# Rebuilding the stored f32 x from its high and low parts in a three-stage kernel (retention, ELU FFN, gated FFN) on one Trainium2 core

## The chip, the cores and the metric

The kernel runs on one core of a Trainium2 chip. The metric is device time in microseconds (us), start to end of one execution; the median of three runs before the change is 871.1 us. Engines are named as in the profile: PE (TensorE matmul), PEld (weight load), DVE (VectorE), ACT (ScalarE), POOL (GpSimd), SP (SyncE, which here only issues DMAs).

## What is computed

```python
def _attn_ref(q, k, v):                  # 4 batches, 8 heads, 576 rows, 64 columns, f32
    scores = np.matmul(q, k.transpose(0, 1, 3, 2)) / sqrt(64)
    gamma = 1.0 - 2.0 ** (-5.0 - np.arange(8))
    Dmat = np.where(rel >= 0, gamma[:, None, None] ** rel, 0.0)
    return np.matmul(scores * Dmat, v)

x = attn_out.transpose(0, 2, 1, 3).reshape(2304, 512)
h = x @ moe_w_in                         # 512 x 2048
x = np.where(h > 0, h, np.exp(np.minimum(h, 0)) - 1) @ moe_w_out
gate = 1 / (1 + np.exp(-(x @ moe2_w_gate)))            # 512 x 1536
out = (gate * (x @ moe2_w_val)) @ moe2_w_out
```

The weights come as 64-bit numbers that are taken apart into f32 on the chip.

## The kernel before

**Precision.** Every f32 operand of a large matmul is kept as a pair: a rounded high part (written by ACT) and the low rest (value minus high part, by DVE or POOL). `mm3` (lines 114 to 116) makes one product of three matmuls: high by high, high by low, low by high. High plus low gives the f32 value back.

**Stages.** Retention runs in 18 steps of 128 rows each (`Step`, `block`), two batches in turn. A step's loads come through SP into one of three `in` buffers or into a borrowed `y` buffer; PE makes scores, sums and outputs (line 274, small 64x64 matmuls), `x_mul` (line 347, DVE) writes the f32 x of the step into an `e` buffer, `x_high` (354, ACT) and `x_low` (361, DVE) split it into `x_of[g]`, where g is the group of four steps (512 rows; group 4 has two steps). For g below 4, `x_low` also sends the f32 x to a DRAM tile `whole[g]` (line 365, 512-byte pieces). Woven in between are the first four of 16 slices of the first FFN (`FF`: `ups`, line 380 or 114 to 116, and, two places later (`LAG`), `downs` into PSUM banks `acc`, emptied by `evac`, lines 440 and 442). The loop over `s` (line 1089) sets that order by hand: `conv[s]` names the weight that is converted there, `loads` the weights requested there, `loads_at` the retention inputs requested in a block, `rest` those that wait until a place's matmuls are done. The places from `begins[1]` (called b, 18) on have 512 columns and no retention any more.

**Pairs of groups.** The other 12 slices of FFN 1 and all of FFN 2 use a seven-product scheme on 2x2 blocks (`Pair`, `product`, `unit`). A pair of row groups needs x blocks "11", "12", "21", "22" and the sums t1 to t4 made of them, each split into high and low. Groups 0 and 1 are the first pair: `prep` loads their four f32 blocks from `whole` into `fs` and `fg` (line 1074) and makes t1 to t4 there (lines 1071, 476, 481, 484). Groups 2 and 3 are the second pair: the split blocks "11", "21", "22" are stored at places b+2 to b+4 (`store`, line 489), t1 to t4 are made later, in the last unit of the first pair, from f32 blocks that `reload` fetches from `whole` (line 992).

**Units.** For each slice pair q from 2 to 7 a `unit_a` runs for the first pair of groups, then again for the second; after that `unit_b` does FFN 2, slice by slice. One unit of the first pair takes 26.5 us. Between a unit's products, `fill` and `bg` put the background work at fixed places: down products, conversions of coming weights (`plan_a`, `plan_b`; `Weight.chain`, lines 154 to 172, with the sums "z" or "s", 196 to 200 and 109, 110), and `hooks`. Converted weights are saved to DRAM tiles `c` (line 1046) and restored for the second pass (1055). `more` (line 961) requests the next raw weight of a list (`feed`) as soon as one of the raw buffers is given back, which is DVE's line 163 of an earlier conversion. Every DMA of these kinds stands in SP's one queue, in program order; a DMA that must wait holds back all behind it.

Of the kernel before, what the change touches and what calls it, by code (L numbers as in the profile page):

```python
# [22 lines left out]
C = 128  # L23
# [20 lines left out]
SPARE = {3: 2, 8: 2, 4: 3, 9: 3, 14: 3}  # L44
LAG = 2
FIRST_APART = 9
WARM = 12, 2, 3, 5, 4, 6


# [5 lines left out]
def retention_elu_glu(  # L55
# [126 lines left out]
    for f in range(FA):  # L182
        for n, src in (("i", w_in), ("o", w_out)):
            i = len(weights)
            W[n, f] = Weight(src[f], i % 8, (0, 0, 1, 1, 0, 1, 0, 1)[i] if i < 8 else t_slot(n, f))
            weights.append(W[n, f])


# [37 lines left out]
    class Step:  # L226
# [16 lines left out]
        def load(self):  # L243
            if self.n in SPARE:
                self.t = spare_y[SPARE[self.n]].rearrange("p (q c) -> p q c", q=NP)
            else:
                self.t = inpool.tile([128, NP, 4 * C], F32, tag="in", name="in")
            self.q, self.kT, self.k, self.v = (self.t[:, :, i * C : i * C + C] for i in range(4))
            if self.last:
                self.load_half(0)  # L250
            elif self.n < FIRST_APART:
                sp.dma_start(out=self.t, in_=ain[self.b, self.c].rearrange("p r x -> r p x"))
            else:
                self.load_pairs(0)
                rest.append(lambda: self.load_pairs(1))
# [4 lines left out]

        def load_half(self, X):
            src = ain[self.b + X, self.c]
            for i in range(2):
                sp.dma_start(out=self.t[:, :, i * C + HC * X : i * C + HC * X + HC],
                             in_=src[:, :, i * C : i * C + HC].rearrange("p q x -> q p x"))
            sp.dma_start(out=self.t[64 * X : 64 * X + 64, :, 2 * C :], in_=src[:, :HC, 2 * C :].rearrange("p t x -> t p x"))

        def scale(self):
            v = self.v.rearrange("t p (h d) -> t p h d", h=2)
# [89 lines left out]

        def x_low(self):  # L360
            dve.tensor_tensor(out=self.x[1], in0=self.xf, in1=self.x[0].bitcast(F32), op=ALU.subtract)
            if self.g < 4:
                if not self.at:
                    whole[self.g] = dpool.tile([128, KB, 512], F32, tag=f"x{self.g}", name="x")
                sp.dma_start(out=whole[self.g][:, :, self.at : self.at + 128], in_=self.xf)


    class FF:
# [78 lines left out]
    class Pair:  # L447
# [2 lines left out]


        HOMES = {"11": (0, 0), "21": (0, 1), "22": (1, 1), "t1": (2, 0), "t2": (2, 1), "t3": (3, 0), "t4": (3, 1)}
        FROM = {"t3": ("22", "12", ALU.subtract), "t2": ("t3", "11", ALU.add), "t1": ("22", "t2", ALU.subtract),
                "t4": ("21", "t2", ALU.subtract)}

# [28 lines left out]
                engine.tensor_tensor(out=p[:, 1, k], in0=self.src[:, k], in1=p[:, 0, k].bitcast(F32), op=ALU.subtract)  # L484

        def store(self, name):
            g, k = {"11": (0, 0), "21": (0, 1), "22": (1, 1)}[name]
            self.halves[name] = dpool.tile([128, 2, KH, 512], F32, tag=f"h{name}", name="h")
            sp.dma_start(out=self.halves[name], in_=x_of[self.g + g][:, :, k * KH : k * KH + KH, :].bitcast(F32))

        def fetch(self, name):
            sp.dma_start(out=self.place(name).bitcast(F32), in_=self.halves[name])
# [309 lines left out]
    with tc.manual_schedule():  # L802
# [50 lines left out]
        for m in range(5, NSTEP):  # L853
            at = {13: 10, 15: 11, 16: 13, 17: 12}.get(m, m - 5)
            loads_at.setdefault(at, []).append(steps[m].load)
        for at, m in ((4, NS - 1), (14, NSTEP - 1)):
            loads_at.setdefault(at, []).insert(0, lambda m=m: steps[m].load_half(1))

        def begin_rest(f):
            while rest:  # L860
                after(rest.pop(0)(), f.end)
# [77 lines left out]
        for i, w in enumerate(weights[4:8]):  # L939
            s = a + 6 + (i * (b - a - 6)) // 4  # L940
            conv[s] = w
            loads.setdefault(s - 2, []).append(w)
        loads.setdefault(b - 7, []).append(W["i", 4])
        for s, n in {-5: ("i", 4), 1: ("i", 5), 2: ("o", 4), 3: ("z", 2), 4: ("o", 5), 5: ("i", 6)}.items():
            conv[b + s] = W[n]

# [11 lines left out]
            feed += [W["2", f]] if f not in EARLY else []  # L958
        feed, last_ones = deque(feed), [W["o", FA - 2], W["o", FA - 1], W["2", FB - 2]]

        def more():
            while raw_free and feed:
                if feed[0] in last_ones and not any(raw_free[0] is r for r in base_raws):
                    if len(raw_free) < 2:
                        return
                    raw_free.rotate(1)
                    if not any(raw_free[0] is r for r in base_raws):
                        return
                feed.popleft().load()
# [19 lines left out]
        def reload(to):  # L989
            for g in (2, 3):  # L990
                to[g] = y_tile(g)
                sp.dma_start(out=to[g], in_=whole[g].rearrange("p k t -> p (k t)"))

        def remake(p):
            return {
# [65 lines left out]
        def prep():  # L1061
            fa, fb = ((lambda t: (t[:, :1024], t[:, 1024:]))(right.tile([128, 2048], F32, tag="s1", name="fs")))
            fc, fd = (right.tile([128, 1024], F32, tag=f"g{i}", name="fg") for i in (4, 5))
            f = {"11": fa, "t2": fa, "12": fb, "t3": fb, "t1": fb, "22": fc, "21": fd, "t4": fd}

            def source(g, k):
                return whole[g][:, k * KH : k * KH + KH, :].rearrange("p k t -> p (k t)")

            def sum(name):
                a, b, op = Pair.FROM[name]  # L1070
                dve.tensor_tensor(out=f[name], in0=f[a], in1=f[b], op=op)

            for name, (g, k) in {"11": (0, 0), "12": (1, 0), "22": (1, 1), "21": (0, 1)}.items():
                sp.dma_start(out=f[name], in_=source(g, k))
            for _ in range(8):
                yield
            for name in ("t3", "t2", "t1", "t4"):
                sum(name)
                yield
                first.high(name, f[name])  # L1080
                yield
                first.low(name, pool if name in ("t3", "t1") else dve)
                yield
                yield
            for name in ("11", "21", "22"):
                first.place(name)

        halves, prepared = None, prep()
        for s in range(end):
# [12 lines left out]
            def stage():  # L1102
                if chain is not None:
                    next(chain, None)
                if s >= begins[1] + 4:
                    next(prepared, None)
            stage()
            if LATE <= s < NSTEP - AHEAD:
# [18 lines left out]
                    stage()  # L1127
            ff[s].ups(stage if s < end - 1 else lambda: None, s, middle, end_)
            if s >= LATE:
                begin_rest(ff[s])  # L1130
            if s == 1:
                w1 = weights[1].chain(dve)
# [22 lines left out]
                begin_rest(ff[s - LAG])  # L1155
            else:
                stage()
            for w in loads.get(s, []):
                load = w.load()
                if s < NSTEP - AHEAD:  # L1160
                    after(load, ff[s - LAG].end)
            save()
            for i, n in enumerate(("11", "21", "22")):
                if s == begins[1] + 2 + i:
                    second.store(n)
            if s == begins[1] + 8:
# [98 lines left out]
        for pair in (first, second):  # L1265
# [3 lines left out]
            for q in range(Q0, QN):  # L1269
                hooks = {}  # L1270
                calls = 7 + len(todo) + (not last_q)
                if not last_q:
# [3 lines left out]
                    if q == QN - 1:  # L1276
                        reload(second.sums)
                        restore(("i", 2 * Q0), ("i", 2 * Q0 + 1), ("z", Q0))
                        p = second
                        hooks = {  # L1280
                            0: [lambda: p.fetch("11")],
                            3: [lambda: p.fetch("21"), lambda: p.sum("t3")],
                            4: [lambda: p.sum("t2")],
                            4.5: [lambda: p.split("t3", dve), lambda: p.sum("t1")],
                            5: [lambda: p.fetch("22"), lambda: p.split("t2", dve)],
                            6: [lambda: p.sum("t4")],
                        }
                    at = (q == Q0 + 1, 1, 2, 3, 4, 4, 6, 6, 7, 7) if len(todo) > 4 else (2, 3, 4, 4)
                else:
                    plan, ahead = ahead[:calls], ahead[calls:]  # L1290
# [15 lines left out]
                    if q + 1 == QN:  # L1306
                        p = y_pair
                        hooks = {
                            1: [lambda: p.high("11")],
                            2: [lambda: p.low("11", dve), lambda: p.sum("t3")],  # L1310
                            4: [lambda: p.sum("t2")],
                            4.5: [lambda: p.split("t3", dve), lambda: p.split("21", pool)],
                            5: [lambda: p.split("t2", dve), lambda: p.sum("t1")],
                        }
                bg = stepper(plan, calls)
                fill = filler(spread(todo, at), bg, hooks)
                unit_a(pair, q, bg, fill, not last_q and q > Q0)
# [26 lines left out]
        for which, pair in enumerate(pairs):  # L1344
            for f in range(FB):
                if not which:
# [5 lines left out]
                    if f == FB - 2:  # L1352
                        unpark((2, 3))
                    plan = plan_b(f)
                else:
                    plan = planned(14)
                back = [(n, f + 1) for n in "vgs" if f + 1 < FB and (which or f + 1 in EARLY)]
# [123 lines left out]
```

## Time and profile before

| | |
|---|---|
| median of 3 runs | 871.1 us (870.54 to 872.78) |
| profiled execution | 868.8 us, span 867.0 us |
| PE | 852.4 us busy, 98% |
| DVE / ACT / POOL | 664.7 / 459.3 / 409.4 us busy |
| DMA | 194.83 MB, mean 225 GB/s |

The profiled execution took 868.8 us, 2.3 us less than the median of the runs shown; its span, 867.0 us, goes from its first to its last instruction. Busy time counts an instruction from start to end, and matmuls overlap, so PE's gaps are read from its waits and from its timeline: 512-column matmuls follow each other there every 0.227 us when nothing holds them. "Issue" as a releaser means that the profile shows nothing that the engine waited for.

### The profile page before, as it was taken

To read this page: it belongs to the slowest core of one execution; us is meant where nothing else is said; L and a number is where in the kernel's file an instruction comes from. 1 tells how busy PE (TensorE), PEld (TensorE's weight loads), DVE (VectorE), ACT (ScalarE), POOL (GpSimd) and SP (SyncE) were. 2 spreads that over 40 slices of the span, in tenths; PEclk is the share of its full clock that TensorE was granted. 3 is DMA by queue.
4 is the path that set the end of the run, shared out by engine and by line. 5 is a ranking of instruction groups with operands and counts; after the bars stand their busy time and mean duration, and the time that the engine had idled before them with its cause. 6 is when DMAs were issued, how large, how long until landed. Compare 5 with 4: busy or idle time off the path is not lost.

```text
span 867.0 us, 16196 instructions
## 1 busy us (share of the span) xinstructions
PE 852.4 (98%) x6375; PEld 728.9 (84%) x6375; DVE 664.7 (77%) x967; ACT 459.3 (53%) x833; POOL 409.4 (47%) x327
## 2 busy tenths in 40 slices
PE   8899999999999999999999999999999999999998
PEld 5798998888888888888878888888888888888886
DVE  5867758789999888887887988589967564777775
ACT  3445475677666666666665665445543344343331
POOL 2445435656546543564552565244543244334453
PEclk9999999999999999999999999999999999999999
DMA  9978628745474696898774765646574665464322
GB/s 339 298 245 245 185 74 314 292 145 202 163 229 184 230 404 227 314 377 274 274 326 176 239 239 210 218 157 196 197 277 157 229 235 194 192 237 170 112 114 98
DMA packets 63852, 194.83 MB, mean 225 GB/s; under 512 B 9888, under 2 KB 19104, under 8 KB 57376
## 3 DMA queue, kind: packets, MB, share of 16 engines
q1 hardware_dynamic: 62512, 192.30, 61.8%
q10 hardware_dynamic: 1264, 1.49, 0.5%
q8 instruction: 50, 0.82, 0.4%
q14 instruction: 26, 0.21, 0.1%
HBM read 127.19 MB, written 66.58 MB: 223 GB/s over the span
## 4 chain that ended last, share of the span: by engine, by line
PE 88%; DVE 4%; DMA 3%; issue 2%; ACT 2%; POOL 1%; SPq 0%; ACTq 0%; DVEq 0%; POOLq 0%
PE u L114 13%; PE u L115 13%; PE u L116 13%; PE acc L114 10%; PE acc L115 10%; PE acc L116 10%; PE tile L114 3%; PE tile L115 3%; PE tile L116 3%; PE to L274 3%; PE h L380 2%; DMA w<-c 2%; PE h L114 1%; PE h L115 1%; PE h L116 1%
## 5 line engine op out<-in xcount | busy, mean ns | idle before, releaser
L110 POOL TENSOR_TENSOR g<-e,g 128x512 fp32r<-128x512 f32 x95 | 133.7, 1412 | 223.8 <-ACT g L109 196.8
L114 PE MATMUL u<-x,s 128*128 128x512 f32 x288 | 112.6, 391 | 0.0
L115 PE MATMUL u<-x,s 128*128 128x512 f32 x288 | 112.3, 390 | 0.0
L116 PE MATMUL u<-x,s 128*128 128x512 f32 x288 | 112.1, 389 | 0.0
L114 PE MATMUL u<-x,w 128*128 128x512 f32 (+1 forms) x264 | 98.3, 372 | 1.5 <-DMA w<-c 1.3
L115 PE MATMUL u<-x,w 128*128 128x512 f32 (+1 forms) x264 | 98.0, 371 | 0.0
L116 PE MATMUL u<-x,w 128*128 128x512 f32 (+1 forms) x264 | 97.7, 370 | 0.0
L109 ACT CAST g<-e 128x512 fp32r<-128x512 f32 x101 | 61.9, 620 | 65.0 <-DVE e L598 39.7
L172 POOL TENSOR_TENSOR w<-t,w 128x512 fp32r<-128x512 f32 x37 | 51.0, 1378 | 41.1 <-ACT w L169 37.5
L114 PEld LDWEIGHTS u<-x,s 128*128 128x128 f32 x288 | 54.1, 188 | 11.5 <-ACT u L522 0.7
L116 PEld LDWEIGHTS u<-x,s 128*128 128x128 f32 x288 | 54.1, 188 | 11.5
L115 PEld LDWEIGHTS u<-x,s 128*128 128x128 f32 x288 | 54.2, 188 | 10.3
L759 DVE TENSOR_TENSOR y<-y,tile 128x512 f32<-128x512 f32 x76 | 51.2, 680 | 10.8 <-PE tile L116 10.6
L114 PE MATMUL acc<-g,w 128*128 128x512 f32 (+1 forms) x168 | 58.2, 346 | 0.4 <-ACT y L440 0.4
L795 DVE TENSOR_TENSOR y<-y,acc 128x512 f32<-128x512 f32 x58 | 39.1, 682 | 25.4 <-PE acc L116 25.0
L114 PEld LDWEIGHTS u<-x,w 128*128 128x128 f32 x264 | 49.8, 189 | 10.2 <-DMA w<-c 1.7
L115 PE MATMUL acc<-g,w 128*128 128x512 f32 (+1 forms) x168 | 57.7, 344 | 0.0
L116 PE MATMUL acc<-g,w 128*128 128x512 f32 (+1 forms) x168 | 57.7, 343 | 0.0
L116 PEld LDWEIGHTS u<-x,w 128*128 128x128 f32 x264 | 49.7, 188 | 8.7
L115 PEld LDWEIGHTS u<-x,w 128*128 128x128 f32 x264 | 49.9, 189 | 7.4
L675 DVE TENSOR_TENSOR y<-y,acc 128x512 f32<-128x512 f32 (+1 forms) x68 | 39.6, 606 | 19.8 <-PE acc L116 17.9
L114 PE MATMUL acc<-w,g 128*128 128x512 f32 (+1 forms) x152 | 54.1, 356 | 0.0
(226 smaller groups left out, 2418.3 us busy)
## 6 DMA issues: line engine op xcount, KB each, us to landing
w<-c SPq DMA_DIRECT2D x72, 512.0 KB, 6.7
c<-w SPq DMA_DIRECT2D x48, 512.0 KB, 4.9
s<-c SPq DMA_DIRECT2D x22, 1024.0 KB, 7.1
c<-s SPq DMA_DIRECT2D x18, 1024.0 KB, 4.9
y<-y SPq DMA_DIRECT2D x8, 1024.0 KB, 6.2
in<-in_ain SPq DMA_DIRECT2D x6, 1024.0 KB, 8.9
raw<-in_w_in SPq DMA_DIRECT2D x12, 512.0 KB, 4.8
in<-in_ain SPq DMA_DIRECT2D x12, 512.0 KB, 5.3
```

Source lines behind the costliest of these rows:

```text
L109: act.copy(hi, src)
L110: lo_engine.tensor_tensor(out=lo, in0=src, in1=hi.bitcast(F32), op=ALU.subtract)
L114: pe.matmul(out_, wh, xh, start=start, stop=False, skip_group_check=shared)
L115: pe.matmul(out_, wh, xl, start=False, stop=False, skip_group_check=shared)
L116: return pe.matmul(out_, wl, xh, start=False, stop=stop, skip_group_check=shared)
L172: lo_engine.tensor_tensor(out=w[:, 1, :], in0=f, in1=w[:, 0, :].bitcast(F32), op=ALU.subtract)
L274: return pe.matmul(out_, w, x, start=start, stop=True, skip_group_check=True)
L380: self.end = pe.matmul(h, w[:, a, c[k]], x[:, b, k, t], start=i + k == 0, stop=i == 2 and k == KB - 1)
L675: dve.tensor_tensor(out=out_, in0=out_, in1=a, op=ALU.add)
L759: dve.tensor_tensor(out=y, in0=y, in1=a, op=ALU.add)
L795: dve.tensor_tensor(out=o, in0=o, in1=a, op=ALU.add)
```

## The change

No step stores its f32 x. `prep` adds high and low of groups 0 and 1 in SBUF instead of loading (two adds on DVE, six on POOL), and its generator starts at place b+2 instead of b+4. For groups 2 and 3, all four split blocks are stored, from b+2 to b+5; in unit q = 3 SP copies the high halves to a DRAM tile `whole[name]`, and in units q = 4 and 5 POOL issues four DMAs that add the low halves onto it; `reload` fetches four 512 KB blocks instead of two of 1 MB. Several requests stand at other places: steps 14 (whole) and 15 and 17 (behind a place's matmuls), the weights 4 to 7 and ("i", 4). Weight 6 uses the other t buffer. The raw loads of ("v", 2) and ("g", 2) are held until the first unit of FFN 2. One split and one sum move from hook 5 to place 12 of the plan of the last `unit_a`.

```diff
+WHOLE, BEHIND = (14,), (15,)
-            W[n, f] = Weight(src[f], i % 8, (0, 0, 1, 1, 0, 1, 0, 1)[i] if i < 8 else t_slot(n, f))
+            W[n, f] = Weight(src[f], i % 8, (0, 0, 1, 1, 0, 1, 1, 1)[i] if i < 8 else t_slot(n, f))
...
             if self.last:
-                self.load_half(0)
-            elif self.n < FIRST_APART:
+                return self.load_half(0)
+            elif self.n in BEHIND:
+                rest.extend(lambda i=i: self.load_pairs(i) for i in range(2))
+            elif self.n < FIRST_APART or self.n in WHOLE:
...
         def x_low(self):
             dve.tensor_tensor(out=self.x[1], in0=self.xf, in1=self.x[0].bitcast(F32), op=ALU.subtract)
-            if self.g < 4:
-                if not self.at:
-                    whole[self.g] = dpool.tile([128, KB, 512], F32, tag=f"x{self.g}", name="x")
-                sp.dma_start(out=whole[self.g][:, :, self.at : self.at + 128], in_=self.xf)
...
+        AT = {"12": (1, 0), "21": (0, 1), "11": (0, 0), "22": (1, 1)}
+        def copy_high(self, name):
+            whole[name] = dpool.tile([128, KH, 512], F32, tag=f"x{name}", name="x")
+            sp.dma_start(out=whole[name], in_=self.halves[name][:, 0])
+
+        def add_low(self, name):
+            pool.dma_start(out=whole[name], in_=self.halves[name][:, 1], accum_op=ALU.add)
+
+        def both(self, name, k, out_, engine):
+            g, h = self.AT[name]
+            hi, lo = (x_of[self.g + g][:, i, h * KH + k, :].bitcast(F32) for i in range(2))
+            engine.tensor_tensor(out=out_[:, k * 512 : k * 512 + 512], in0=hi, in1=lo, op=ALU.add)
...
-        for at, m in ((4, NS - 1), (14, NSTEP - 1)):
-            loads_at.setdefault(at, []).insert(0, lambda m=m: steps[m].load_half(1))
+        loads_at.setdefault(4, []).insert(0, lambda: steps[NS - 1].load_half(1))
+        loads_at[12] = [lambda: rest.append(steps[NSTEP - 1].load)]
+        loads_at[14] = [lambda: rest.append(lambda: steps[NSTEP - 1].load_half(1))]
...
-            loads.setdefault(s - 2, []).append(w)
-        loads.setdefault(b - 7, []).append(W["i", 4])
+            loads.setdefault((4, 6, 7, 13)[i], []).append(w)
+        loads.setdefault(10, []).append(W["i", 4])
...
+        waiting = [W[n, 2] for n in "vg"]
+
         def more():
-            while raw_free and feed:
+            while raw_free and feed and feed[0] not in waiting:
...
-                sp.dma_start(out=to[g], in_=whole[g].rearrange("p k t -> p (k t)"))
+            for name in ("22", "12", "11", "21"):
+                sp.dma_start(out=second.f32(name), in_=whole[name].rearrange("p k t -> p (k t)"))
...
-            for name, (g, k) in {"11": (0, 0), "12": (1, 0), "22": (1, 1), "21": (0, 1)}.items():
-                sp.dma_start(out=f[name], in_=source(g, k))
-            for _ in range(8):
+            for name in ("12", "22", "11", "21"):
+                for k in range(KH):
+                    first.both(name, k, f[name], dve if name == "12" else pool)
+                    yield
+                    if name != "12":
+                        yield
+            for _ in range(2):
                 yield
...
-                if s >= begins[1] + 4:
+                if s >= begins[1] + 2:
                     next(prepared, None)
...
             if s >= LATE:
+                rest.extend(w.load for w in loads.get(s, []))
                 begin_rest(ff[s])
...
-            for i, n in enumerate(("11", "21", "22")):
+            for i, n in enumerate(second.AT):
                 if s == begins[1] + 2 + i:
                     second.store(n)
...
+                    if q in (Q0 + 1, Q0 + 2, Q0 + 3):
+                        by = (second.copy_high, second.add_low)[q > Q0 + 1]
+                        hooks = {j: [lambda n=n, by=by: by(n)] for j, n in zip((1, 3, 5, 6), second.AT) if q == Q0 + 1 or (j < 4) == (q == Q0 + 2)}
...
-                            5: [lambda: p.split("t2", dve), lambda: p.sum("t1")],
                         }
+                        plan[12] = [lambda: p.split("t2", dve), lambda: p.sum("t1"), *plan[12]]
...
+                    if not f:
+                        plan[3] += [waiting.clear, more]
```

The order of PE's instructions is the same before and after. Two places show what moves on the others. First, DVE from the last evacuation of group 4's first pass on (place b+1) to the evacuation before which PE needs the next two banks. Before:

```order
L440 COPY y_2294<-acc 128x256 x2
L157 TENSOR_SCALAR t<-t 128x512
L158 TENSOR_SCALAR t<-t 128x512
L161 ISA t<-raw,t 128x1024
L397 SCALAR_TENSOR_TENSOR e<-e,h 128x512
L163 SCALAR_TENSOR_TENSOR t<-raw,t 128x512
L196 TENSOR_TENSOR t<-t 128x256
L197 TENSOR_TENSOR t<-t 128x256
L199 TENSOR_TENSOR t<-t 128x256
L200 TENSOR_TENSOR t<-t 128x256
L397 SCALAR_TENSOR_TENSOR e<-e,h 128x512
L442 TENSOR_TENSOR y_2294<-y_2294,acc 128x256 x4
```

With the change:

```order
L439 COPY y_2273<-acc 128x256 x2
L501 TENSOR_TENSOR fs<-x_116 128x512
L158 TENSOR_SCALAR t<-t 128x512
L159 TENSOR_SCALAR t<-t 128x512
L501 TENSOR_TENSOR fs<-x_116 128x512
L162 ISA t<-raw,t 128x1024
L396 SCALAR_TENSOR_TENSOR e<-e,h 128x512
L164 SCALAR_TENSOR_TENSOR t<-raw,t 128x512
L197 TENSOR_TENSOR t<-t 128x256
L198 TENSOR_TENSOR t<-t 128x256
L200 TENSOR_TENSOR t<-t 128x256
L201 TENSOR_TENSOR t<-t 128x256
L396 SCALAR_TENSOR_TENSOR e<-e,h 128x512
L441 TENSOR_TENSOR y_2273<-y_2273,acc 128x256 x4
```

The two `fs<-x` rows are high plus low of block "12"; they stand around the two shifts and scalings of a weight's conversion, ahead of all that follows up to the four `y<-y,acc`. On POOL six more such adds stand between the rows behind it.

Second, SP in the last unit before FFN 2 (`w<-c` and `s<-c` restore weights, `c<-x` and `c<-s` save them, `raw` are raw loads). Before:

```order
L1055 DMA w<-c 128x1024 x2
L144 DMA raw<-in_w_val 128x1024
L1055 DMA w<-c 128x1024
L1046 DMA c<-x_116 128x1024
L144 DMA raw<-in_w_gate 128x1024
L1046 DMA c<-x_116 128x1024
L1055 DMA s<-c 128x2048
L1055 DMA w<-c 128x1024 x2
L1046 DMA c<-s 128x2048
L1055 DMA w<-c 128x1024 x2
L1046 DMA c<-x_116 128x1024
L1055 DMA w<-c 128x1024 x2
```

With the change:

```order
L1071 DMA w<-c 128x1024 x3
L1062 DMA c<-x_116 128x1024 x2
L1071 DMA s<-c 128x2048
L1071 DMA w<-c 128x1024 x2
L1062 DMA c<-s 128x2048
L1071 DMA w<-c 128x1024 x2
L1062 DMA c<-x_116 128x1024
L1071 DMA w<-c 128x1024
L145 DMA raw<-in_w_val 128x1024
L145 DMA raw<-in_w_gate 128x1024
L1071 DMA w<-c 128x1024
```

The raw loads of `w_val` and `w_gate` leave the places ahead of the two saves `c<-x`, the restore `s<-c` and all behind them, and stand after the fifth `w<-c` that follows.

## Rows read from the trace of the kernel before

**Rows 1.** The page: span, and PE's busy time.
```profile
span 867.0 us, 16196 instructions
...
PE 852.4 (98%) x6375; PEld 728.9 (84%) x6375; DVE 664.7 (77%) x967; ACT 459.3 (53%) x833; POOL 409.4 (47%) x327
```

**Rows 2.** Waits of PE: total us, times, longest us.
```profile
PE to L274 <- issue: 1.4, 2, 1.2
...
PE u L114 <- DMA w<-c: 1.3, 1, 1.3
...
PE h L380 <- issue: 0.9, 1, 0.9
...
PE acc L114 <- ACT y L440: 0.4, 1, 0.4
...
PE ts L274 <- issue: 0.3, 1, 0.3
```

**Rows 3.** PE's timeline in a late retention step: start us, us, [idle before <-releaser].
```profile
81.28 0.63 PE L274 MATMUL to<-in 64*64 64x64 f32 x29
83.10 0.27 PE L274 MATMUL to<-in 64*64 64x64 f32 x1 [1.19 <-issue]
```

**Rows 4.** Windows: us, busy per engine (x), PEclk, DMA share, GB/s.
```profile
40.00:110.00 70.00, 68.02 (x1759) 64.73 (x1759) 48.27 (x86) 35.66 (x86) 35.27 (x38) 1.00 0.74 224
...
215.50:242.00 26.50, 26.50 (x139) 22.61 (x138) 24.52 (x35) 18.24 (x33) 15.56 (x12) 1.00 0.57 197
...
421.00:428.40 7.40, 7.40 (x34) 6.13 (x33) 7.26 (x10) 2.48 (x5) 3.56 (x3) 1.00 0.26 104
430.50:444.40 13.90, 12.59 (x56) 10.10 (x54) 12.09 (x12) 10.35 (x16) 11.26 (x8) 1.00 1.01 409
```

**Rows 5.** DMA issues: count, KB each, median us to landing.
```profile
w<-c SPq DMA_DIRECT2D x72, 512.0 KB, 6.7
...
x<-e SPq DMA_DIRECT2D x14, 256.0 KB, 4.7
```

**Rows 6.** ACT's timeline, conversion of ("i", 4).
```profile
102.27 0.68 ACT L154 ACTIVATE t<-raw 128x512 f32<-128x512 f32 x1 [1.40 <-POOL w L172]
```

**Rows 7.** Timelines of DVE, POOL and PE around place b+2.
```profile
128.56 1.06 DVE L157 TENSOR_SCALAR t<-t 128x512 f32<-128x512 f32 x1 [0.60 <-ACT t L154]
...
132.01 0.42 DVE L196 TENSOR_TENSOR t<-t 128x256 f32<-128x256 f32 x1
...
133.91 1.40 DVE L199 TENSOR_TENSOR t<-t 128x256 f32<-128x256 f32 x1
...
137.26 1.40 DVE L442 TENSOR_TENSOR y<-y,acc 128x256 f32<-128x256 f32 x4
...
128.04 1.30 POOL L172 TENSOR_TENSOR w<-t,w 128x512 fp32r<-128x512 f32 x1 [0.31 <-ACT w L169]
...
137.78 0.44 PE L114 MATMUL acc<-g,w 128*128 128x512 f32 x1
```

**Rows 8.** DVE's groups from 20 to 460 us: busy us, mean ns | idle before.
```profile
L361 DVE TENSOR_TENSOR x<-e,x 128x512 fp32r<-128x512 f32 x16 | 12.1, 755 | 5.3 <-ACT x L354 5.3
```

**Rows 9.** SP's waits: total us, times, longest us.
```profile
SPq L144 <- DVE t L163: 180.4, 37, 11.1
```

**Rows 10.** Timelines of POOL, SP and PE before the first unit of FFN 2.
```profile
419.13 2.56 POOL L172 TENSOR_TENSOR x<-t,x 128x512 fp32r<-128x512 f32 x2 [3.39 <-ACT x L169]
...
420.45 0.32 SPq L1046 DMA_DIRECT2D c<-x  x1
428.09 0.33 SPq L144 DMA_DIRECT2D raw<-in_w_gate  x1
428.52 0.38 SPq L1046 DMA_DIRECT2D c<-x  x1
...
434.53 0.93 SPq L1055 DMA_DIRECT2D w<-c  x2
...
444.41 0.50 PE L114 MATMUL u<-x,w 128*128 128x512 f32 x1 [1.32 <-DMA w<-c]
```

More of the change, by code (lines that the diff above doesn't have):

```diff
@@ L262, in load_half @@
             src = ain[self.b + X, self.c]
-            for i in range(2):
-                sp.dma_start(out=self.t[:, :, i * C + HC * X : i * C + HC * X + HC],
-                             in_=src[:, :, i * C : i * C + HC].rearrange("p q x -> q p x"))
+            first, _ = [sp.dma_start(out=self.t[:, :, i * C + HC * X : i * C + HC * X + HC],
+                                     in_=src[:, :, i * C : i * C + HC].rearrange("p q x -> q p x")) for i in range(2)]
             sp.dma_start(out=self.t[64 * X : 64 * X + 64, :, 2 * C :], in_=src[:, :HC, 2 * C :].rearrange("p t x -> t p x"))
+            return first
         def scale(self):
@@ L486, in store @@
         def store(self, name):
-            g, k = {"11": (0, 0), "21": (0, 1), "22": (1, 1)}[name]
+            g, k = self.AT[name]
             self.halves[name] = dpool.tile([128, 2, KH, 512], F32, tag=f"h{name}", name="h")
             sp.dma_start(out=self.halves[name], in_=x_of[self.g + g][:, :, k * KH : k * KH + KH, :].bitcast(F32))
+        def copy_high(self, name):
[7 more added lines that the diff above has]
+            engine.tensor_tensor(out=out_[:, k * 512 : k * 512 + 512], in0=hi, in1=lo, op=ALU.add)
         def fetch(self, name):
@@ L1064, in prep @@
             f = {"11": fa, "t2": fa, "12": fb, "t3": fb, "t1": fb, "22": fc, "21": fd, "t4": fd}
-            def source(g, k):
-                return whole[g][:, k * KH : k * KH + KH, :].rearrange("p k t -> p (k t)")
             def sum(name):
@@ L1157, in retention_elu_glu @@
                 stage()
[L1158 to L1161, printed above, removed]
             save()
-            for i, n in enumerate(("11", "21", "22")):
+            for i, n in enumerate(second.AT):
                 if s == begins[1] + 2 + i:
```

## The prediction

> **What bounds the kernel now.** I read the page first. PE is busy for 852.4 of 867.0 us [rows 1], and the change neither adds nor removes nor reorders a matmul. So the change can win back only gaps of PE, some 14.6 us in all, and can lose by making new ones. The list of PE's waits says where the gaps are [rows 2]: apart from the start-up before 40 us, which the change hardly touches, PE waits 1.3 us for a restored weight, 1.4 and 0.3 us for nothing that the profile names ("issue"), and 0.4 us for an evacuation by ACT. PE's timeline shows the largest nameless gap [rows 3]: 29 of 32 equal small matmuls run at once, and the last waits 1.19 us. Nothing in the program tells that matmul from the others, so what was late is likely the instructions themselves, which also come by DMA. Last, the windows [rows 4]: from 40 to 110 us, 68.02 of 70 us of PE are busy, so 1.98 us is all that the retention steps can give. In that stretch the DMA engines are 0.74 busy; between 430.5 and 444.4 us they are full (1.01, at 409 GB/s).
>
> **Stores of x that go.** Sixteen stores of 256 KB leave SP; fourteen of them are in one row [rows 5], 4.7 us to landing each. 16 x 0.262 is 4.2 MB, and 70 us at 224 GB/s [rows 4] are 15.7 MB, so about a quarter of the traffic of the stretch goes. PE waits for no store and no input there [rows 2], so shorter transfers are worth nothing by themselves. What they may be worth is the nameless gaps: 1.19 us [rows 3] and 0.3 us [rows 2]. I take both as gone: -1.19 - 0.3 = **-1.5 us**. Bounds: 0 if they have another cause, and -2.4 us if the 0.9 us nameless gap of the start-up [rows 2], where stores are also in flight, goes too. Inputs and weights that are asked for elsewhere cost nothing while a whole step lies between request and use; PE's 1.98 us of gaps hold no wait for an input. If that cover were gone, one late request costs at most about a landing, 4.7 us [rows 5].
>
> **Other t buffer for weight 6.** Before, ("i", 4) uses the same buffer right behind weight 6, and ACT waits 1.40 us for POOL to finish with it [rows 6]. ACT, then DVE, are late from there on until PE waits 0.4 us for ACT's evacuation [rows 2]. With the other buffer that chain has 1.40 us more room: **-0.4 us**; at worst 0.
>
> **Blocks made in SBUF by prep.** Four loads of 512 KB go, and eight adds come. Six on POOL at about 1.30 us [rows 7] are 7.8 us. At most two of them stand between one g and the next on POOL, so a g comes up to 2.6 us later; PE uses it two places on, 10.9 us later (48 matmuls at 0.227 us). I take that as hidden; all six ahead of one g, 7.8 us, would still be. The two on DVE are another matter. DVE has a single idle of 0.60 us there, before 128.56, and from then on works without a pause (no row has an idle before it) to the evacuation at 137.26, whose first quarter PE awaits at 137.78 [rows 7]: the first of the four parts takes 1.40 / 4 = 0.35 us and so ends at 137.61, 0.17 us before PE uses its bank. PE has next to no room. One such add costs about 0.755 us (same size, both inputs in SBUF [rows 8]). Two are 1.5 us less the idle 0.60: 0.9 us at least, if nothing is stretched. But DVE's work there is stretched beside POOL: two adds of 128x256 take 0.42 and 1.40 us [rows 7]. If both new ones took 1.40 us, the price were 2 x 1.40 - 0.60 = 2.2 us. I take **+1.2 us**, nearer the low end, because 0.755 us is a mean over sixteen, of which some ran beside POOL already. The Trainium skill speaks against this part too: "SBUF — State Buffer", section "Who interferes with whom", says that a DVE instruction with two SBUF inputs contends with a GpSimd instruction that reads SBUF. By that rule alone the price would be the upper end, 2.2 us, and the whole forecast 1.0 us later; the pair 0.42 and 1.40 agrees with the rule, the mean of 0.755 says that not every add pays.
>
> **Fourth store, copies, accumulating DMAs, reload.** The fourth store (1 MB) takes less than the four loads that go (2 MB) in the same stretch. Four copies on SP and four additions issued by POOL come at units q = 3 to 5, where the DMA share is 0.57 [rows 4]; the data are used in unit 7, two units later. On SP they delay no restore there. On POOL the trace has no DMA at all. Bounds: nothing, since in a unit POOL is idle for 26.50 - 15.56 = 10.9 us [rows 4]; or POOL is held until the data have landed, which is the second rival. I take **0**, as an issue on SP holds the queue for 0.3 to 0.4 us [rows 10]. By the Trainium skill ("DMA: Bandwidth & Descriptors", section "Latency and other measured facts") the first byte of a GpSimd DMA comes after about 1 us of emission; by that four cost POOL some 4 us of idle time and the sum stays as it is. The reload in four parts moves as many bytes as in two: 0.
>
> **Held raw loads and moved split.** Before 444.41 PE waits 1.32 us for a weight restore that SP issues at 434.53 [rows 10], into full DMA engines [rows 4]. Just before, from 421 to 428.4, the DMA share is 0.26 [rows 4]: SP's queue stands at the raw load of `w_gate`, issued at 428.09 only, the kind of request that waits for DVE to give back a raw buffer [rows 9]. Behind it stands a save `c<-x`, whose data POOL has finished at 419.13 + 2.56 = 421.7 [rows 10]. With the change the raw load is not there, and the save can start some 6.8 us earlier, in the quiet stretch. So at least 2 x 0.524 = 1.05 MB no longer lie ahead of the late restore; at 409 GB/s that is 2.6 us, twice the wait. **-1.3 us**; bound 0, if the restores behind wait for PE to free their slots, so that nothing but the save comes earlier (0.52 MB, 1.3 us, would still just do). The held loads are issued behind the fifth restore and have until place 11 of 14 of the next unit before they are converted; uncovered they would cost one landing, 6.7 us [rows 5]. The moved split puts a product's add ahead of a split on DVE, in a stretch with no wait of PE before 444.41: 0.
>
> **Sum.** -1.5 - 0.4 + 1.2 + 0 - 1.3 = -2.0 us: the profiled execution of 868.8 us would take 866.8 us. It stands 2.3 us below the median of the runs, 871.1 us; so I put the new median at 871.1 - 2.0 = **869.1 us**, 0.23% less. A measurement of this kernel can tell about 0.3%, 2.6 us, from no change; the forecast lies within it.
>
> **Rivals.**
> *The adds cost nothing.* If DVE takes them up in idle time or the evacuation has more room than the rows show, the gains stand alone: -3.2 us, 867.9 us; with the start-up gap -4.1 us, 867.0 us. For: one idle of 0.60 us is there, and DVE works ahead of PE in other places. Against: no pause from 128.56 to 137.26 [rows 7].
> *POOL is held by its DMAs* (slower). If POOL stands still until its addition has landed, two per unit at 6.7 us (the nearest row of that size, [rows 5]) take 13.4 us out of 10.9 us of idle time: PE is late by 2.5 us per unit, 5.0 us in two, and -2.0 + 5.0 = +3.0 us: 874.1 us. It decides from 10.9 / 2 = 5.5 us per DMA. For: no row shows POOL issuing. Against: no other queue is held for a transfer; SP's rows are 0.3 to 0.5 us each [rows 10].
> *The nameless gaps stay.* The stores go, but the gap of 1.19 us and its like stay or come elsewhere in the retention steps, or a late input takes their place: -2.0 + 1.5 = -0.5 us, 870.6 us. That the gain of the stores isn't there is also how the change would fail to do what it says. For: PE waits for no data there, so nothing proves that the DMA load is the cause. Against: the gap stands among equal matmuls, in a stretch of 0.74 DMA share. The Trainium skill ("Runtime: NRT & Kernel Launch", section "Instruction fetch mechanics") says that the next block of instructions is fetched while the last one runs and that this is mostly hidden; by that rule this rival would hold. The trace shows the gap, and not what it is.
>
> **How the numbers follow.** Forecast 0.38, adds free 0.38, gaps stay 0.14, POOL held 0.10. Forecast and third rival lie within 2.6 us of 871.1, but for an edge of the forecast (0.02 of it, where the adds cost 0.9 us or less); the first rival is faster, the second slower. So faster 0.40, same 0.50, slower 0.10. The range reaches down to the first rival with the start-up gap, 867.0, less a little for the spread of the runs, 866.8; up to the third rival with adds at their upper end, 870.6 + 1.0 = 871.6, and 0.6 for the spread of the runs: 872.2. It leaves out the POOL case and the ends.
>
> **What would show it.** Right: no gap of PE before 444 us and a DMA share in 421 to 428 well above 0.26; no nameless gap near 82 us; no wait of ACT for POOL near 102 us; one new wait of PE for DVE's line of the evacuation near 138 us, about 1 us long. Wrong: PE waiting for g or a weight of POOL between 215 and 268 us; a nameless gap elsewhere before 110 us; no wait near 138 us.

## The result, and the profile after

The changed kernel takes **875.22 us** (median of 9 runs, 873.73 to 879.68) against 871.17 us for the kernel before in the same session (9 runs, 868.91 to 873.30): ratio 1.0052, 95% interval 1.0032 to 1.0072. It is slower by about 4 us; the forecast was 869.1 us, and the range ended at 872.2.

The profiled execution of the changed kernel took 875.54 us. Its page, the lines that answer to [rows 1]:

```profile
span 873.8 us, 16170 instructions
...
PE 854.7 (98%) x6375; PEld 730.7 (84%) x6375; DVE 673.9 (77%) x969; ACT 459.0 (53%) x833; POOL 421.5 (48%) x337
```

PE has the same 6375 matmuls and is "busy" 2.3 us longer. The waits of PE, as in [rows 2] (total us, times, longest us):

```profile
PE acc L115 <- DVE y L441: 4.5, 2, 3.0
...
PE to L277 <- issue: 1.0, 1, 1.0
...
PE tile L116 <- POOL g L111: 0.6, 1, 0.6
PE acc L115 <- ACT y L439: 0.5, 1, 0.5
PE tile L115 <- DVE y L771: 0.5, 1, 0.5
```

The wait of 1.3 us for a restored weight is gone, the nameless wait left is in the start-up (30.27 us), and there are 4.5 us that were not there: two waits for the evacuations of places b+3 and b+5 (places b and b+1 still have 256 columns, those from b+2 on 512). PE's timeline at both:

```profile
138.12 0.50 PE L115 MATMUL acc<-g,w 128*128 128x512 f32 x1 [1.49 <-DVE y L441]
...
152.32 0.80 PE L115 MATMUL acc<-g,w 128*128 128x512 f32 x1 [3.00 <-DVE y L441]
...
157.61 0.63 PE L115 MATMUL h<-x,w 128*128 128x512 f32 x1
158.04 0.51 PE L116 MATMUL h<-x,w 128*128 128x512 f32 x1
```

From 152.32 to 158.04 us PE does 13 matmuls in 5.72 us, 0.44 us each instead of 0.227: 2.8 us more. The windows say why, and show where POOL and DVE stand (columns as in [rows 4]):

```profile
40.00:110.00 70.00, 69.09 (x1802) 65.77 (x1801) 51.24 (x88) 36.25 (x89) 36.94 (x40) 1.00 0.59 180
135.00:140.00 5.00, 3.51 (x16) 2.59 (x15) 4.93 (x9) 2.82 (x5) 5.00 (x5) 1.00 1.01 404
140.00:145.00 5.00, 5.00 (x24) 4.04 (x23) 4.55 (x4) 1.58 (x4) 5.00 (x4) 1.00 0.44 181
145.00:150.00 5.00, 4.33 (x20) 3.25 (x18) 3.91 (x3) 2.57 (x5) 4.92 (x4) 1.00 0.85 297
150.00:155.00 5.00, 2.67 (x6) 2.17 (x7) 5.00 (x8) 0.62 (x1) 1.27 (x1) 0.64 0.37 94
155.00:160.00 5.00, 5.00 (x16) 3.96 (x15) 2.70 (x3) 2.80 (x4) 3.57 (x3) 0.67 1.03 421
190.00:420.00 230.00, 229.87 (x1132) 193.51 (x1131) 201.30 (x277) 152.93 (x266) 126.50 (x90) 1.00 0.78 273
```

From 40 to 110 us PE's gaps are 0.9 us instead of 1.98 [rows 4]. Behind the wait of 3.00 us the granted clock is 0.64 and 0.67 over two windows, that is, part of each at 1.2 GHz. From 135 to 150 us POOL works 14.92 of 15 us. What that does to DVE stands in their timelines, DVE first:

```profile
139.87 1.40 DVE L159 TENSOR_SCALAR t<-t 128x512 uint32<-128x512 uint32 x1
141.39 1.58 DVE L162 CUSTOM_DVE_ANT_0 t<-raw,t 128x1024 uint16<-128x1024 uint16 x1
...
143.49 1.18 DVE L164 SCALAR_TENSOR_TENSOR t<-raw,t 128x512 uint32<-128x512 uint32 x1
145.93 1.44 DVE L158 TENSOR_SCALAR t<-t 128x512 f32<-128x512 f32 x1 [1.26 <-ACT t L155]
...
148.91 1.56 DVE L162 CUSTOM_DVE_ANT_0 t<-raw,t 128x1024 uint16<-128x1024 uint16 x1
...
151.60 1.27 DVE L441 TENSOR_TENSOR y<-y,acc 128x512 f32<-128x512 f32 x2
```

```profile
142.38 1.74 POOL L501 TENSOR_TENSOR fs<-x 128x512 f32<-128x512 f32 x1
144.08 1.74 POOL L501 TENSOR_TENSOR fg<-x 128x512 f32<-128x512 f32 x1
```

Two conversions stand ahead of the evacuation `y<-y,acc` on DVE, and nearly every step of them runs beside a POOL instruction. The evacuation of four parts starts at 151.60 us (the row shows two of them); PE waits for the first.

### The profile page after: what moved, and what is told of

Same layout as the page of the kernel before. It is cut to its first block, busy times and chain, and to the rows that moved or that the text cites. A ratio compares the mean times of both kernels' runs of the same rounds, so it can differ in the third digit from the quotient of the medians.

```text
span 873.8 us, 16170 instructions
## 1 busy us (share of the span) xinstructions
PE 854.7 (98%) x6375; PEld 730.7 (84%) x6375; DVE 673.9 (77%) x969; ACT 459.0 (53%) x833; POOL 421.5 (48%) x337
## 3 DMA queue, kind: packets, MB, share of 16 engines
q10 hardware_dynamic: 1264, 1.49, 0.5%
## 4 chain that ended last, share of the span: by engine, by line
PE 81%; DVE 11%; ACT 4%; issue 2%; DMA 1%; POOL 0%; SPq 0%; DVEq 0%; ACTq 0%; POOLq 0%
PE u L115 13%; PE u L116 13%; PE u L117 13%; PE acc L115 9%; PE acc L116 9%; PE acc L117 9%; PE tile L115 3%; PE tile L117 3%; PE tile L116 3%; PE to L277 3%; PE h L379 1%; DVE t L158 1%; DVE t L159 1%; DVE t L162 1%; DMA raw<-in_w_in 1%
## 5 line engine op out<-in xcount | busy, mean ns | idle before, releaser
L115 PE MATMUL acc<-g,w 128*128 128x512 f32 (+1 forms) x168 | 58.9, 351 | 5.0 <-DVE y L441 4.5
L117 PE MATMUL acc<-g,w 128*128 128x512 f32 (+1 forms) x168 | 58.4, 347 | 0.0
L116 PE MATMUL acc<-g,w 128*128 128x512 f32 (+1 forms) x168 | 58.3, 347 | 0.0
```

Of the source, the lines that this page charges most:

```text
L115: pe.matmul(out_, wh, xh, start=start, stop=False, skip_group_check=shared)
L116: pe.matmul(out_, wh, xl, start=False, stop=False, skip_group_check=shared)
L117: return pe.matmul(out_, wl, xh, start=False, stop=stop, skip_group_check=shared)
```

## The experiments

**Which adds cost it.** Three kernels leave out adds of prep and load those blocks from an input instead; a fourth makes all eight sums by DMA. The cut shows the first of the three; in the second `loaded` is ("22", "11", "21"), in the third ("12",).

```diff
+loaded = ("12", "22", "11", "21")
+for i, name in enumerate(loaded):
+    sp.dma_start(out=f[name].rearrange("r (p x) -> r p x", p=2), in_=ain[0, i, 2:4].rearrange("p r x -> r p x"))
 for name in ("12", "22", "11", "21"):
     for k in range(KH):
-        first.both(name, k, f[name], dve if name == "12" else pool)
+        if name not in loaded:
+            first.both(name, k, f[name], dve if name == "12" else pool)
```

> Leaves out: the eight adds high + low of groups 0 and 1; the four blocks of prep are instead loaded (512 KB each, by SP) from an input, so the sums t1 to t4 of the first pair are made of other numbers. All else is the changed kernel, no step stores its x. Theory (the eight adds cost the time): no PE wait for the evacuation near 138 and 152 us, no slow matmuls behind it; PE's gaps fall by 1.49 + 3.00 = 4.5 us and the slow matmuls' 2.7 us go too: 875.2 - 7.2 = 868.0 us. Rival (the earlier start of prep, the fourth store or the moved requests cost it): the 3.00 us wait stays and the time with it, 873 to 875 us.

> Leaves out: the six adds on POOL (blocks 11, 21, 22 are loaded from an input instead, 512 KB each); the two adds on DVE stay. Theory (POOL's adds stretch DVE's conversions): the wait near 138 us stays at about 1.2 us, the one near 152 us and the slow matmuls behind it go: 875.2 - 3.0 - 2.7 = 869.5 us. Rival (the two DVE adds delay the whole chain and POOL's adds are harmless): both waits stay, 874 to 875 us.

> Leaves out: the two adds on DVE (block 12 is loaded from an input instead); the six adds on POOL stay. Theory (POOL's adds stretch DVE's conversions): the wait near 138 us goes or falls below 0.5 us, the one near 152 us stays at 1.5 to 3 us with slow matmuls behind it: 871.5 to 874 us. Rival (the two DVE adds are the cause): both waits go, 868 to 869 us.

| | median, us (runs) | ratio to before, 95% interval | PE waits near 138 / 152 us |
|---|---|---|---|
| changed kernel | 875.22 (9) | 1.0052 (1.0032 to 1.0072) | 1.49 / 3.00 |
| no adds | 870.73 (10) | 0.9984 (0.9964 to 1.0003) | none / none |
| two on DVE alone | 869.79 (10) | 0.9989 (0.9972 to 1.0007) | 0.54 / none |
| six on POOL alone | 874.64 (10) | 1.0034 (1.0017 to 1.0052) | 1.12 / 2.97 |

The waits went and stayed as the theory said, except that the one near 138 us stays at 1.12 us without the two DVE adds (below 0.5 expected): most of it is POOL's doing, too. The slow matmuls that were expected behind 2.97 us are not there, and two of the times missed: 870.73 us without adds (868.0 expected) and 874.64 us with POOL's six (at most 874). The same four DVE instructions in both kernels, first with DVE's two adds alone, then with POOL's six alone:

```profile
130.28 0.43 DVE L159 TENSOR_SCALAR t<-t 128x512 uint32<-128x512 uint32 x1
...
141.62 0.69 DVE L162 CUSTOM_DVE_ANT_0 t<-raw,t 128x1024 uint16<-128x1024 uint16 x1
...
144.78 0.51 DVE L158 TENSOR_SCALAR t<-t 128x512 f32<-128x512 f32 x1 [1.26 <-ACT t L155]
...
146.85 0.69 DVE L162 CUSTOM_DVE_ANT_0 t<-raw,t 128x1024 uint16<-128x1024 uint16 x1
```

```profile
128.30 1.40 DVE L159 TENSOR_SCALAR t<-t 128x512 uint32<-128x512 uint32 x1
...
140.97 1.57 DVE L162 CUSTOM_DVE_ANT_0 t<-raw,t 128x1024 uint16<-128x1024 uint16 x1
...
145.51 1.43 DVE L158 TENSOR_SCALAR t<-t 128x512 f32<-128x512 f32 x1 [1.26 <-ACT t L155]
...
148.50 1.56 DVE L162 CUSTOM_DVE_ANT_0 t<-raw,t 128x1024 uint16<-128x1024 uint16 x1
```

The first row of each stands ahead of the evacuation near 138 us: 0.43 becomes 1.40 us, against the wait of 1.12 us. The other three stand ahead of the one near 152 us: 0.69 becomes 1.57 and 1.56 us, 0.51 becomes 1.43 us. That is 2.7 us; two more instructions of that stretch (0.45 to 0.82 and 0.69 to 1.19 us) make it 3.5 us, against the wait of 2.97 us. By medians the eight adds cost 875.22 - 870.73 = 4.5 us. The kernel without adds is not measurably faster than the kernel before: its interval reaches down to 0.9964, 3.1 us, and the forecast gave the other parts of the change 3.2 us. The runs further down look for where that went.

```diff
-        first.both(name, k, f[name], dve if name == "12" else pool)
...
+for name in ("12", "22", "11", "21"):
+    sp.dma_start(out=to(name), in_=part(name, 0))
+for _ in range(8):
+    yield
+for name in ("12", "22", "11", "21"):
+    pool.dma_start(out=to(name), in_=part(name, 1), accum_op=ALU.add)
+    yield
```

Here `part(name, 0)` is the high half of a block in SBUF, `part(name, 1)` the low one, and `to(name)` the block of prep.

> Computes everything. The eight adds are made by DMA: SP copies the high halves of the four blocks within SBUF, POOL issues four DMAs that add the low halves onto them, as the changed kernel does in DRAM for groups 2 and 3. Theory (an add on DVE or POOL costs, an issue on POOL does not): POOL is held about 0.95 us per issue (as at 223.35 us in the changed kernel), no wait near 138 or 152 us: 868 to 869 us, the changed kernel's gains alone. Rival (POOL is held, or its descriptor work stretches DVE as its adds do): a wait near 152 us of 1 us or more, 870 to 873 us.

Measured: 871.49 us (10 runs), ratio 1.0010 (0.9992 to 1.0028). The wait near 138 us is gone, near 149 us one of 0.98 us is left. The expected 868 to 869 us were not reached; they counted on gains that the kernel without adds (870.73 us) does not have either. The row of DVE that is late there, and the issue of POOL beside it:

```profile
142.71 3.01 DVE L158 TENSOR_SCALAR t<-t 128x512 f32<-128x512 f32 x1 [1.25 <-ACT t L155]
```

```profile
142.89 1.20 POOL L1096 DMA_DIRECT2D fg<-x  x1
143.50 1.92 POOL L173 TENSOR_TENSOR w<-t,w 128x512 fp32r<-128x512 f32 x1
```

The instruction that takes 0.51 us in the kernel with two adds on DVE takes 3.01 us here, from just ahead of POOL's issue to about the end of POOL's next split (145.72 and 145.42 us). Beside POOL's first three issues, from 139.10 us on, no instruction of DVE is longer than in the kernel with two adds on DVE; so what held this one is not shown. Four issues of POOL are cheaper than six adds; that they are free for DVE, one execution can't say.

**Where the expected gains went.**

> The kernel before, unchanged, profiled once more. It tells which of PE's gaps are the kernel's and which are one execution's. Theory (the nameless gaps and the start-up differ from run to run): the gaps at 83.10 and 99.2 us and the waits before 40 us differ by up to 1 to 2 us from the first profile, and so says nothing that the changed kernel lacks one; the named waits at 107.65 (0.41, ACT) and 444.41 us (1.32, DMA) are there again within 0.2 us. Rival (the nameless gaps come from the DMA load of the stores): 1.19 us near 83 us and 0.28 us near 99 us again.

```diff
 def more():
-    while raw_free and feed:
+    while raw_free and feed and feed[0] not in waiting:
...
+if not f:
+    plan[3] += [waiting.clear, more]
```

> The kernel before with one part of the change: the raw loads of (v, 2) and (g, 2) are held until the first unit of FFN 2; the split and the sum stay at hook 5. Theory (the held loads remove the wait and the moved split makes the two new ones): no wait for a restore near 444 us, and none near 452 or 458 us: -1.3 us there. Rival (the units are that tight, so that the time won at 444 us is lost to the next chain anyway): waits of about 0.6 and 0.5 us near 452 and 458 us.

```diff
+5: [lambda: p.split("t2", dve), lambda: p.sum("t1")],
...
-plan[12] = [lambda: p.split("t2", dve), lambda: p.sum("t1"), *plan[12]]
```

> The changed kernel with the split of t2 and the sum t1 of the last unit_a back at hook 5. Theory (the moved split makes the two new waits): the waits of 0.58 us near 453 (POOL g) and 0.46 us near 459 us (DVE y) go, -1.0 us; those near 138 and 152 us stay. Rival: both waits stay, or the wait for a restore near 444 us comes back.

```diff
-plan[12] = [lambda: p.split("t2", dve), lambda: p.sum("t1"), *plan[12]]
+plan[12] = [lambda: p.split("t2", dve), *plan[12]]
...
-(0, 0): remake_more(p0, x_last),
+(0, 0): {**remake_more(p0), 0: [lambda: p0.sum("t1"), lambda: p0.split("22", dve)], 5: [x_last]},
```

> Computes everything. The changed kernel with the sum t1 moved out of the last unit_a to the start of the first unit of FFN 2, and the split of group 4's x there from hook 2 to hook 5. Theory (DVE, which makes the sum of 2.3 us ahead of the ELU step of that unit, is what PE waits for through POOL's g): the wait of 0.58 us near 453 us goes, the one near 459 us stays or goes; those near 138 and 152 us stay. Rival (the g is late for another reason): both stay.

The four were run and profiled once each (869.68, 872.14, 878.23 and 873.22 us, in this order), so they are compared by their waits and not by their times. PE's rows, first of the kernel before, a second time:

```profile
84.01 0.27 PE L274 MATMUL to<-in 64*64 64x64 f32 x1 [2.07 <-issue]
...
445.54 0.50 PE L114 MATMUL u<-x,w 128*128 128x512 f32 x1 [1.44 <-DMA w<-c]
```

The wait for the restore is there again, 1.44 us; the nameless gap is 2.07 us where it was 1.19 [rows 3]. In the eleven other profiled executions it was 2.05 us (no adds), 2.11 (two on DVE), 2.48 (held loads, below) and 2.35 us (hook put back, below), and 0.75 us or less, or absent, in seven. Of the four, three have no stores of x: the gap comes without them, too. It was small or absent in seven of ten executions without the stores and in none of three with them; whether the stores make it more frequent stays open.

Then the kernel before with the held loads, the changed kernel with the hook put back, and with the sum late:

```profile
451.02 0.50 PE L115 MATMUL tile<-g,w 128*128 128x512 f32 x1 [1.55 <-POOL g L110]
```

```profile
456.55 0.50 PE L116 MATMUL tile<-g,w 128*128 128x512 f32 x1 [1.55 <-POOL g L111]
```

```profile
451.76 0.50 PE L116 MATMUL tile<-g,w 128*128 128x512 f32 x1 [0.59 <-POOL g L111]
```

Holding the loads does remove the wait for the restore; PE then arrives 1.3 to 1.4 us earlier and waits 1.55 us for a g of POOL. In the kernel before, POOL is as slow with these two g, but PE comes later and does not wait:

```profile
443.03 4.50 POOL L110 TENSOR_TENSOR g<-e,g 128x512 fp32r<-128x512 f32 x2
```

The moved split and sum are not the cause of the two new waits of the changed kernel, as I had thought: without the move they are one longer wait (1.55 instead of 0.58 + 0.46). With the sum late the second wait goes (0.46), the first stays at 0.59; so that theory fell for the first. In this last kernel the chain of waits ahead of 451.76 us runs through POOL, whose timeline has no pause there from 445.46 us on:

```profile
445.46 2.77 POOL L484 TENSOR_TENSOR x<-y,x 128x512 fp32r<-128x512 f32 x2 [2.47 <-ACT x L476]
448.19 3.52 POOL L111 TENSOR_TENSOR g<-e,g 128x512 fp32r<-128x512 f32 x2
```

A split of an x block, which had itself waited 2.47 us for its high part from ACT, stands ahead of two g. The two g take 3.52 us, and one alone, at 441.70 us, 1.29 us; DVE is at work beside them for most of that time. Whether taking the split from POOL removes the wait was not tried.

The wait near 107 us for ACT's evacuation, in the changed kernel, rows of PE, ACT, POOL and DVE:

```profile
106.34 0.39 PE L115 MATMUL acc<-g,w 128*128 128x256 f32 x1 [0.54 <-ACT y L439]
```

```profile
99.87 0.67 ACT L155 ACTIVATE t<-raw 128x512 f32<-128x512 f32 x1
...
102.01 1.50 POOL L274 TENSOR_TENSOR in<-in,small 128x512 f32<-128x512 f32 x1
...
102.52 1.27 DVE L158 TENSOR_SCALAR t<-t 128x512 f32<-128x512 f32 x1
```

ACT no longer waits for POOL [rows 6]. But the conversion now comes to DVE beside POOL's scaling of an input: its first instruction takes 1.27 us there (0.42 us in the kernel before, at 104.67 us), and the room that was won is used up again. PE waits 0.54 us instead of 0.41. That is not a loss: in the second execution of the kernel before the wait was 0.20 us, in the kernel with the held loads, which is the same up to there, 0.90 us, and 0.53 or 0.54 us in all ten executions with the change.

**Other places for the adds.**

```diff
+if s == begins[1] - 2:
+    ret.close()
...
+turns = [(name, k) for k in range(KH) for name in ("12", "11")] + [(name, k) for k in range(KH) for name in ("22", "21")]
+for name, k in turns:
+    by = dve if name in ("12", "22") else pool
+    first.both(name, k, f[name], by)
...
-if s >= begins[1] + 2:
+if s >= begins[1] - 1:
```

`ret.close()` gives up the SBUF of the retention steps, in which prep's blocks then lie; the next kernel does so one place sooner still.

> Computes everything. The changed kernel with the eight adds made earlier: the retention steps' SBUF is given up three places sooner, the adds (12 and 22 on DVE, 11 and 21 on POOL) run in places b-1 to b+1, from about 116 to 126 us, where in the kernel before DVE and POOL are idle more than half of the time; prep's sums stand where they stood. Theory (what costs is that POOL works without pause beside DVE's conversions in the places in which DVE has no room): no PE wait of over 0.3 us near 138 and 152 us and no slow matmuls: 868 to 870.5 us. Rival (the adds only move the stretch): a wait of 0.5 us or more for g, for a weight or for an evacuation between 116 and 140 us, 871 us or more.

Measured: 873.59 us (12 runs), ratio 1.0024 (1.0010 to 1.0038). The rival held. PE's new wait, and what stands ahead of it on DVE and POOL:

```profile
130.66 0.39 PE L115 MATMUL acc<-g,w 128*128 128x256 f32 x1 [2.12 <-DVE y L439]
```

```profile
125.64 1.77 DVE L501 TENSOR_TENSOR fg<-x 128x512 f32<-128x512 f32 x1
127.33 1.78 DVE L162 CUSTOM_DVE_ANT_0 t<-raw,t 128x1024 uint16<-128x1024 uint16 x1
...
125.39 3.17 POOL L501 TENSOR_TENSOR fg<-x 128x512 f32<-128x512 f32 x2
```

Where an add of POOL and one of DVE meet, DVE's takes 1.77 us and POOL's two 3.17 us (0.74 us at 117.83 and 1.29 us for one at 119.14 us in the same kernel), and the conversion behind them is long, too.

```diff
+if s == begins[1] - 3:
+    ret.close()
...
+for name in ("12", "22", "11", "21"):
+    for k in range(KH):
+        first.both(name, k, f[name], dve)
+        yield
...
+if s >= begins[1] - 2:
```

> Computes everything. The changed kernel with all eight adds on DVE, none on POOL, between about 115 and 124 us (from place b-2 on, for which the retention steps' SBUF is given up at the end of place b-3), where DVE has 7 us without work; prep's sums stand where they stood. Theory (POOL's adds beside DVE's conversions are what costs; an add on DVE in idle time with POOL left alone costs nothing): each add takes about 0.7 us, no PE wait of over 0.3 us between 112 and 160 us: 869.5 to 871 us, like the run without adds. Rival (any add delays the evacuations behind it): a wait near 128 to 131 us of 0.5 us or more, 871.5 us or more.

> Computes everything. Both of the two edits before in one kernel: all adds early on DVE, and the sum t1 late. Theory: the named waits near 138, 152, 453 and 459 us are gone, so 4.5 + 1.0 us below the changed kernel's 875.2 us: 869 to 870 us, 1 to 2 us below the kernel before. Rival (what is won at one place is waited for at the next): 871 us, the same as before.

Measured: 870.86 us (12 runs), ratio 0.9999 (0.9983 to 1.0015), and with the late sum as well 870.94 us (12 runs), 0.9996 (0.9982 to 1.0010). With POOL left alone, the eight adds take 0.7 to 0.9 us each on DVE, and PE waits 0.40 us near 130 and 0.77 us near 140 us, where none over 0.3 us was expected; the time lies in the range of the theory. With the late sum as well, the rival held: 871 us and not 869 to 870, and the wait for POOL's g is still there (0.59 us). Both kernels are some 4.4 us below the changed kernel, and the same as the kernel before: no version tried here beats it. In both kernels (and in the one without adds) the profiled execution has a granted clock of 0.54 to 0.58 from 30 to 35 us, behind gaps of the start-up, where the kernel before had 1.00 both times; whether that belongs to these kernels or to those executions stays open.

## Why the prediction was wrong

**Blocks made in SBUF by prep** is the step that failed, and in it the sentence on POOL: six adds "I take that as hidden". I had looked only at who waits for POOL's own results. They do come in time. But while POOL works without pause, instructions of DVE's conversions take 1.4 to 1.6 us instead of 0.4 to 0.7 us, and it was DVE that had no room ahead of the evacuations; I had said so myself a few sentences later and had priced it for the two new DVE adds alone. For these I took +1.2 us, out of bounds from 0.9 to 2.2; they measured 0.54 us alone. With all eight the wait near 138 us was 1.49 us, and the second, 3.00 us, near the evacuation two places on, was in no term. The rule that I weighed there (the Trainium skill, "SBUF — State Buffer", section "Who interferes with whom") holds for a DVE instruction with two SBUF inputs against a GpSimd instruction that reads SBUF; the conversions' row of 0.69 against 1.57 us agrees. I applied it to the added instructions and not to those that were there already. The rows of 0.51 against 1.43 us and 0.43 against 1.40 us have one input and are not covered by it; what stretches them beside POOL, these runs don't show.

**Slow matmuls** were in no term either: 2.8 us in the profiled execution, behind the wait of 3.00 us. They are not in every execution, and the change costs as much without them: two of the nine runs had a mean granted clock of 0.999 and 1.000 (0.993 in the profiled one) and took 875.22 us, which is the median, and 874.60 us.

**Stores of x that go**, -1.5 us: not shown. The gap is one execution's; it comes with and without the stores. I had given "the gaps stay" 0.14, and read 1.19 us from a single execution as a property of the kernel. That the changed kernel's profile shows no gap near 82 us, as I had listed for "right", is luck of that execution.

**Other t buffer**, -0.4 us: the wait of ACT went as said, the wait of PE did not (0.20 to 0.90 us in three executions without the change, 0.53 or 0.54 in ten with it): DVE beside POOL took the room back.

**Held raw loads**, -1.3 us: the mechanism was right, with the DMA share from 421 to 428.4 us as said:

```profile
421.00:428.40 7.40, 7.40 (x34) 6.15 (x33) 5.57 (x8) 5.73 (x11) 3.95 (x4) 1.00 0.89 363
430.50:444.40 13.90, 13.90 (x63) 11.52 (x62) 12.39 (x17) 7.21 (x13) 8.93 (x6) 1.00 0.62 225
```

0.89 instead of 0.26, then 0.62 instead of 1.01 [rows 4], and no wait at 444. What I left out was the next chain: 0.58 + 0.46 = 1.04 us came back at 453 and 459 us, and 1.55 us where the part stands alone. I had called the moved split 0 because no wait stood there; none stood there because PE came later.

**Fourth store, copies, accumulating DMAs**, 0: right. POOL is held 0.81 to 0.95 us per issue in those units, and PE has 229.87 of 230 us from 190 to 420 us. The rival "POOL is held by its DMAs" is out:

```profile
223.35 0.95 POOL L496 DMA_DIRECT2D x<-h  x1
```

The sum as it came, from one profiled execution to the other: 1.49 + 3.00 + 2.8 for the adds and what follows them, -1.32 + 1.04 at the held loads, +0.1 at 107 us, together 7.1 us; they are 875.54 - 868.8 = 6.7 us apart, and the difference is gaps that are another length in every execution. By medians the change costs 875.22 - 871.17 = 4.05 us, the adds 4.5 us, and all else nothing that can be told from zero. All the signs that I had listed for "right" came, the wait near 138 us among them at 1.49 us; the list had no line for a wait at a place that I had not worked out.

## What to carry to other kernels

Before work is put on an idle POOL, look at what DVE does at that time: where DVE has no room ahead of something that PE waits for, POOL's instructions are paid by DVE's. When a wait of PE is removed, follow each chain on to the next one that was covered by it, and don't book a gap that was seen in one execution only.

## What the runs showed that I had not expected

A wait of PE of about 3 us can cost up to nearly twice its length. It came in four profiled executions at the same place, and the matmuls behind it together took 2.8, 1.7, 1.7 and about 0 us longer than at 0.227 us each. Behind 3.00 us (changed kernel) the granted clock was 0.67 over 155 to 160 us, behind 2.97 us (hook put back) 0.66 over the same stretch, behind 2.94 us (sum late) 0.72 over 150 to 155 us, and behind 2.97 us (POOL's six alone) 1.00 throughout:

```profile
155.00:160.00 5.00, 4.14 (x11) 3.32 (x12) 3.73 (x6) 1.49 (x3) 1.38 (x2) 0.66 0.61 200
```

```profile
150.00:155.00 5.00, 3.09 (x14) 2.56 (x15) 4.79 (x8) 0.80 (x2) 1.28 (x1) 1.00 0.45 124
```

The first row is the kernel with the hook put back, the second the one with POOL's six adds alone. What decides between them, these runs don't show.
